# One copied score of every second phase is exponentiated on GpSimd, and the scores of a phase are dealt out anew

## The chip, the cores and the metric

The kernel runs on one core of a Trainium2 chip. The metric is the device time of one execution in microseconds (us); before the change it is 1262.92 us, the median of three runs (1262.78 to 1262.97).

## What is computed

A gate mixes two branches that read the same x (2048 tokens of 512 channels, float32):

```python
qkv = (x @ wqkv).reshape(B, S, 3, H, Dh)       # H = 32 heads, Dh = 16
p = softmax(einsum("bhqd,bhkd->bhqk", q, k) * Dh**-0.5)
a = einsum("bhqk,bhkd->bhqd", p, v).transpose(...).reshape(B, S, D) @ wo
u = gelu(einsum("bsd,sf->bdf", layernorm(x), w1) + b1)      # F = 1792
b = (einsum("bdf,fs->bds", u, w2) + b2).transpose(...)
out = g * a + (1 - g) * b                       # g = sigmoid((x * gate_w).sum(-1))
```

The attention needs 32 x 2048 x 2048 exponentials, and they are most of what follows.

## The kernel before, in words

**Ahead of the attention** come the projections, the layer norm and the first layer of the mixer branch. The change does not touch them.

**The attention** is a loop of 128 phases, p = 0 to 127, written out in the order in which each engine runs its work; no scheduler moves anything there. Four phases make a group: two heads against one half (1024) of the queries. The place of a phase in its group is called 0, 1, 2 or 3 here (`ph` in the code); places 1 and 3 are the `second` phases. A phase forms sixteen scores, each of 128 keys by 512 queries, numbered n = 0 to 15, and it has three stretches of TensorE work:

- sixteen score matmuls (L1067). Beside the first 14 (or 12) runs, on the other 64 rows of the array, half of a *dense* matmul (L1076) of other work: the second mixer layer, the queries of the second half (`late_query`), the output projection. Even phases do one half of these matmuls, odd phases the other, into one bank `dn`. A one-element GpSimd memset `token` (L1080), called the fence, stands between two phases: it waits for a phase's last dense matmul, and the next phase's first dense matmul waits for it.
- the last two scores, which run side by side without dense work.
- the matmuls with V (L963), which add all sixteen exponentiated scores into one PSUM bank `av`. VectorE then adds that bank to the running sum `ot` in SBUF (L985).

**Who takes a score out of PSUM.** Before the change, ScalarE exponentiates six scores one by one straight out of PSUM (`SINGLE`, n = 0, 2, 4, 6, 7, 9; L1093) and four in two pairs of 1024 columns (`TWO`; L1031). VectorE copies six (`EVAC`, n = 1, 3, 5, 8, 14, 15; L1089) into one SBUF tile `pe` of 3072 columns, and ScalarE exponentiates these in one instruction (L1102). The copied scores are used one phase later (`held`), the others in their own phase.

**Banks.** Seven PSUM banks go round for scores and `av`; the eighth is `dn`. A score matmul waits until the bank that it gets has been read. Worked through by hand, the rule `shares` gives this in all 128 phases: score 14 takes the bank of the fifth single (n = 7), score 15 that of the fourth copy (n = 8), and `av` that of the sixth single (n = 9).

**Sums at a group's edge.** In place 0, the held scores of the old group close its sum, and then the new group's first scores go to a second bank. VectorE adds the closing bank while the second is being filled; the second bank's addition stands at the head of the next phase, ahead of its copies.

**Around it on VectorE.** After its copies, an odd phase also empties a finished `dn` (L542, L816, or the five steps of `late_query`, L616 to L630), splits the next block of `w2` into a high part (`w_hi`, L67) and hands the low part to GpSimd (`w_lo`, L68, a subtraction of two SBUF tiles). Now and then come the reciprocals of the row sums (`inv`, L755 and L756) and the scaling and splitting of finished heads (`fetch`, `load_wo`, L1119 and L67/L68), most of them in the last sixteen phases.

The four lines that take scores out:

```python
nc.vector.tensor_copy(pt, s)                                              # L1089, EVAC
one = nc.scalar.activation(pt, s, AF.Exp, scale=SCALE)                    # L1093, SINGLE
pairs_done.append(nc.scalar.activation(pt, twos[low, low + 1], AF.Exp, scale=SCALE))   # L1031, TWO
done = nc.scalar.activation(x, x, AF.Exp, scale=SCALE)                    # L1102, the copied ones
```

Of the kernel before, what the change touches and what calls it, by code (L numbers as in the profile page):

```python
# [23 lines left out]
P = 128  # L24
# [33 lines left out]


@with_exitstack  # L60
def gated_mix(ctx: ExitStack, tc: tile.TileContext, a_x, a_wqkv, a_wo, b_w1, b_b1, b_w2, b_b2, gate_w, out):
# [38 lines left out]
    const.tile([P, 16], F32, name="pad")  # L100
# [501 lines left out]
    wq, between = [], {}  # L602

    def late_query(b, n):
# [9 lines left out]
        def begin():  # L614
            box.append(out_pool.tile([P, D], F32, name="row", bufs=3))
            nc.vector.tensor_copy(box[-1].bitcast(F32R), box[2])  # L616

        def out():
            ps, hi, cols = box[2], box[-1], slice((n - 2) * NB, (n - 1) * NB)
            lo, most_k = (out_pool.tile([P, D], F32, name="row", bufs=3) for _ in range(2))  # L620
            nc.vector.tensor_tensor(lo.bitcast(F32R), ps, hi, ALU.subtract)
            nc.vector.tensor_scalar(most_k, ps, most[:, b : b + 1], None, ALU.mult)
            nc.vector.tensor_reduce(qmax[:, b, n : n + 1], ps, axis=AX.X, op=ALU.max, apply_absolute_value=True)
            for i, t in enumerate((hi, lo)):
                nc.sync.dma_start(qp_d[1][b][i, :, cols], t)
            box.extend((most_k, qp_d[1][b][2, :, cols]))

        def finish():
            most_k, dst = box[-2:]
            nc.vector.scalar_tensor_tensor(most_k.bitcast(F32R), most_k, -1.0, most_k, ALU.mult, ALU.max)  # L630
            nc.sync.dma_start(dst, most_k)

        between[out] = begin
# [8 lines left out]
        return [(step, k, j) for k in range(ND) for j in range(3)], load, finish  # L642

    def second_layer(t):
# [3 lines left out]
        def step(fc, k):  # L648
            if fc == 0 and k == 0:
                box.append(ps_dn.tile([P, D], F32, name="dn"))  # L650
            if fc % 4 == 0 and k == 0:
                load_weight()
                box.append(ready.pop(0))
# [92 lines left out]
    def invert(half, k, pairs, at):  # L746
# [4 lines left out]
        t = out_pool.tile([P, w], F32, name="inv")[: n * DH]  # L751
# [97 lines left out]
    def put_whole(what, at):  # L849
        steps, load, *finish = what  # L850
        call(2 * at - 2, load)
        if finish:
            on_dve(2 * at + 2, *finish)
# [23 lines left out]
    for t in range(NS):  # L877
        at = put(second_layer(t), at, [14] * 3)
        if queries:
# [4 lines left out]
            if (b, n) == (ND - 1, 3):  # L884
                call(2 * at, open_wo)
                on_dve(2 * at + 1, greatest_of_all)
                call(2 * at + 2, bring_most)
                on_dve(2 * at + 4, least_shifts)
# [27 lines left out]
    token, mark = (out_pool.tile([1, 1], F32, name=name, bufs=1) for name in ("token", "mark"))  # L916

    EVAC = 1, 3, 5, 8, 14, 15
    SINGLE = 0, 2, 4, 6, 7, 9
    TWO = (10, 11), (12, 13)  # L920
    TURNS = [(0, 2), (4, 6), (7, 9), *TWO]
    HELD = [(1, 3), (5, 8), (14, 15)]

    def shares(n):

        for one in range(0, BANKS, 2):
            lows = [k for k in range(one)][::2] + [k for k in range(one + 1, BANKS)][::2]
            for third in lows:
                if n in (third, third + 1):
                    first, second = (low for low in lows if low != third)  # L930
                    return [first, first + 1, one, second, second + 1, 2 * third + 1 - n, n]


    def regions():
        return tc.tile_pool(name="ps_s", bufs=1, space=PSUM, reuse_waits="tile")
# [54 lines left out]
    with tc.manual_schedule(engines=engines):  # L990
        held, fence, turn, spare = [], None, 0, 0
        landed.clear()

        for p in range(LAST + 1):
# [17 lines left out]
            head = [second if n < n_b else (second + NSC - 1 - n) % 2 for n in range(NSC)]  # L1012
            if n_b == NSC - 2:
                head[-2:] = second, 1 - second
            else:
                head[-4:] = second, 1 - second, 1 - second, second
            in_turn = list(range(n_b)) + ([14, 15] if n_b == NSC - 2 else [12, 13, 15, 14])
# [9 lines left out]
            def exps(n):  # L1027
# [283 lines left out]
```

## Time and profile before

| what | value |
|---|---|
| median of three runs | 1262.92 us |
| the profiled execution's own time | 1262.86 us |
| its span in the profile | 1261.1 us |
| TensorE, busy share of the span | 99% |
| ScalarE, busy share | 85% |
| VectorE, busy share | 67% |
| GpSimd, busy share | 16% |
| granted TensorE clock | 1.0 |

The attention loop starts at 275.5 us of the span and its last score is formed at 1222 us, so it is three quarters of the time. In the stretch from 300 to 1100 us both TensorE and ScalarE are shown busy all the time. The ends of matmuls are modelled, and instructions of ScalarE overlap in the profile (the next is shown to start while the one before is still in the pipeline), so a share of 100% says only that an engine never stood empty; what it can do at most is read from the distance between the starts of its instructions.

### The profile page before, as it was taken

To read this page: it belongs to the slowest core of one execution; us is meant where nothing else is said; L and a number is where in the kernel's file an instruction comes from. 1 tells how busy PE (TensorE), PEld (TensorE's weight loads), DVE (VectorE), ACT (ScalarE), POOL (GpSimd) and SP (SyncE) were. 2 spreads that over 40 slices of the span, in tenths; PEclk is the share of its full clock that TensorE was granted. 3 is DMA by queue.
4 is the path that set the end of the run, shared out by engine and by line. 5 is a ranking of instruction groups with operands and counts; after the bars stand their busy time and mean duration, and the time that the engine had idled before them with its cause. 6 is when DMAs were issued, how large, how long until landed. Compare 5 with 4: busy or idle time off the path is not lost.

```text
span 1261.1 us, 32707 instructions
## 1 busy us (share of the span) xinstructions
PE 1253.0 (99%) x13342; PEld 827.9 (66%) x13342; DVE 850.8 (67%) x1562; ACT 1068.7 (85%) x1405; POOL 199.2 (16%) x316
## 2 busy tenths in 40 slices
PE   9999999999999999999999999999999999999998
PEld 7888888875666666666666666666666666666656
DVE  5675453178767676667667677776777677678883
ACT  4453343269999999999999999999999999999990
POOL 0220444561011101010110101111111111000000
PEclk9999999999999999999999999999999999999999
DMA  4799443253754443534344433444543443367621
GB/s 130 249 341 330 146 124 108 80 139 109 207 126 102 88 100 83 160 84 97 85 100 94 105 87 79 93 86 81 116 99 77 86 100 60 56 165 174 152 61 70
DMA packets 100555, 152.31 MB, mean 121 GB/s; under 512 B 17109, under 2 KB 56171, under 8 KB 96300
## 3 DMA queue, kind: packets, MB, share of 16 engines
q1 hardware_dynamic: 99820, 149.08, 46.6%
q8 instruction: 107, 1.75, 0.6%
q10 hardware_dynamic: 576, 1.05, 0.2%
q14 instruction: 52, 0.43, 0.1%
HBM read 105.39 MB, written 44.68 MB: 119 GB/s over the span
## 4 chain that ended last, share of the span: by engine, by line
PE 99%; ACT 1%; DVE 0%; issue 0%
PE av L963 32%; PE s L1067 23%; PE acc L424 12%; PE t L1067 9%; PE acc L75 8%; PE t L963 5%; PE u L1067 3%; PE dn L1076 3%; PE pa L1162 2%; PE acc L199 1%; PE acc L268 1%; PE acc L245 0%; ACT p L1093 0%; ACT pe L1102 0%; PE dn L1162 0%; PE pa L1192 0%
## 5 line engine op out<-in xcount | busy, mean ns | idle before, releaser
L1093 ACT ACTIVATE p<-s 128x512 f32<-128x512 f32 x768 | 412.3, 790 | 0.1
L1102 ACT ACTIVATE pe<-pe 128x3072 f32<-128x3072 f32 x129 | 381.8, 2962 | 0.0
L1067 PE MATMUL s<-qs,ks 64*128 64x512 f32 x1280 | 330.0, 400 | 0.6 <-ACT p L1093 0.6
L1089 DVE COPY pe<-s 128x512 f32<-128x512 f32 x512 | 318.1, 683 | 4.8 <-PE s L1067 0.8
L1067 PEld LDWEIGHTS s<-qs,ks 64*128 64x128 f32 x1280 | 225.6, 184 | 95.4 <-issue 45.3
L1031 ACT ACTIVATE p<-t 128x1024 f32<-128x1024 f32 x256 | 278.4, 1265 | 0.0
L963 PE MATMUL av<-p,v 128*32 128x256 f32 x3880 | 227.2, 379 | 0.0
L1089 DVE COPY pe<-u 128x512 f32<-128x512 f32 x256 | 164.8, 686 | 72.1 <-PE u L1067 72.1
L963 PE MATMUL av<-pe,v 128*32 128x256 f32 x3072 | 192.5, 383 | 0.0
L985 DVE TENSOR_TENSOR ot<-av,ot 128x512 f32<-128x512 f32 (+2 forms) x160 | 93.1, 582 | 141.5 <-PE av L963 140.2
L68 POOL TENSOR_TENSOR w_lo<-w_raw,w_hi 128x512 fp32r<-128x512 f32 (+1 forms) x128 | 153.5, 1206 | 194.5 <-ACT w_hi L67 101.8
L1076 PE MATMUL dn<-u_lo,w_hi 64*128 64x512 f32 x448 | 180.8, 404 | 0.0
L1076 PE MATMUL dn<-u_hi,w_hi 64*128 64x512 f32 x448 | 180.7, 403 | 0.0
L963 PEld LDWEIGHTS av<-p,v 128*32 128x32 f32 x3880 | 126.1, 110 | 83.2 <-ACT p L1093 0.2
L1076 PE MATMUL dn<-u_hi,w_lo 64*128 64x512 f32 x448 | 180.7, 403 | 0.0
L1067 PE MATMUL t<-qs,ks 64*128 64x512 f32 x512 | 142.5, 413 | 0.0
L963 PEld LDWEIGHTS av<-pe,v 128*32 128x32 f32 x3072 | 86.8, 109 | 82.1 <-ACT p L1093 37.8
L1080 POOL MEMSET token<- 1x1 f32 x128 | 11.3, 88 | 742.4 <-PE dn L1076 720.5
L67 ACT CAST w_hi<-w_raw 128x512 fp32r<-128x512 f32 (+1 forms) x67 | 38.0, 570 | 80.9 <-PE acc L424 59.4
L1067 PEld LDWEIGHTS t<-qs,ks 64*128 64x128 f32 x512 | 72.9, 184 | 51.2 <-ACT p L1093 49.9
L424 PE MATMUL acc<-h_hi,w_hi 128*128 128x512 f32 x224 | 87.1, 389 | 0.0
L424 PE MATMUL acc<-h_lo,w_hi 128*128 128x512 f32 x224 | 87.1, 389 | 0.0
(171 smaller groups left out, 1615.0 us busy)
## 6 DMA issues: line engine op xcount, KB each, us to landing
w_raw<-in_B_w_dram SPq DMA_DIRECT2D x96, 256.0 KB
ks<-kp SPq DMA_DIRECT2D x192, 128.0 KB
qs<-qp SPq DMA_DIRECT2D x256, 64.0 KB
kp<-pc SPq DMA_DIRECT2D x16, 512.0 KB
qp<-pc SPq DMA_DIRECT2D x8, 768.0 KB
qp<-row SPq DMA_DIRECT2D x24, 256.0 KB
v<-v SPq DMA_DIRECT2D x4, 1088.0 KB
x<-in_A_x_dram SPq DMA_DIRECT2D x16, 256.0 KB
```

The source lines that it names most:

```text
L67: copy(hi, src)
L68: return sub(lo, src, hi.bitcast(F32), ALU.subtract)
L75: nc.tensor.matmul(ps, a, b, start=start and n == 0, stop=stop and n == last)
L424: nc.tensor.matmul(p, a, b, start=first and k == 0, stop=last and k == 2)
L963: mm = nc.tensor.matmul(av[32 * j : 32 * (j + 1), i * QC : (i + 1) * QC], vb[b][:, v_at : v_at + 32], pt[:, h * QC : (h + 1) * QC], start= ...
L985: latest["add"] = nc.vector.tensor_tensor(x, y, x, ALU.add)
L1031: pairs_done.append(nc.scalar.activation(pt, twos[low, low + 1], AF.Exp, scale=SCALE))
L1067: nc.tensor.matmul(s, kt[grp][rows_i, c * P : (c + 1) * P], qt[grp][rows_i, qb * NB : (qb + 1) * NB], start=True, stop=True,)
L1076: mm = nc.tensor.matmul(ps, a[half], b[half], start=begin and not second, stop=last and bool(second))
L1089: nc.vector.tensor_copy(pt, s)
L1093: one = nc.scalar.activation(pt, s, AF.Exp, scale=SCALE)
L1102: done = nc.scalar.activation(x, x, AF.Exp, scale=SCALE)
```

## The change

It does five things.

1. **Shares.** `KINDS` deals the sixteen scores out as "sesesesseesessaa": ScalarE takes eight singles (n = 0, 2, 4, 6, 7, 10, 12, 13) and one pair (14, 15), VectorE six copies (n = 1, 3, 5, 8, 9, 11).
2. **GpSimd.** In even phases (`on_pool`), score 1 is not copied into `pe`. VectorE takes it out of PSUM scaled by log2(e)/4 into the tile `by` (L1159 of the changed kernel). GpSimd splits it into a whole and a broken part and builds 2 to the whole part from exponent bits (`powers`, four instructions), and after the fence begins a polynomial of the broken part (`polynomial`, six instructions). In the next, odd phase VectorE finishes it with two instructions that read two SBUF tiles each (`product`), after its copies, and the result goes to the V matmuls of that phase, in the last pair. ScalarE's instruction on the copied scores has 2560 columns in even phases and 3072 in odd ones.
3. **Banks** come from a table, `GIVEN`, one row a phase: the banks of the sixteen scores, then of `av`. Worked through by hand, all 128 rows give the following: the pair (14, 15) takes the banks of the fifth single (n = 7) and the fourth copy (n = 8), and `av` that of the sixth single (n = 10).
4. **Late queries.** VectorE copies the finished `dn` to SBUF at once, and the four other steps read that SBUF copy, spread over the next three phases.
5. **Small things.** `w_raw` has three buffers instead of four; three instructions around the bound of the scores are two phases later; `token` and `mark` lie elsewhere.

The diff, cut to its core:

```diff
-            raw = wk.tile([P, NB], F32, name="w_raw", bufs=4)
+            raw = wk.tile([P, NB], F32, name="w_raw", bufs=3)
...
         def out():
-            ps, hi, cols = box[2], box[-1], slice((n - 2) * NB, (n - 1) * NB)
-            lo, most_k = (out_pool.tile([P, D], F32, name="row", bufs=3) for _ in range(2))
-            nc.vector.tensor_tensor(lo.bitcast(F32R), ps, hi, ALU.subtract)
-            nc.vector.tensor_scalar(most_k, ps, most[:, b : b + 1], None, ALU.mult)
-            nc.vector.tensor_reduce(qmax[:, b, n : n + 1], ps, axis=AX.X, op=ALU.max, apply_absolute_value=True)
...
+            raw = out_pool.tile([P, D], F32, name="row", bufs=3)
+            nc.vector.tensor_copy(raw, box[2])
+            box.append(raw)
+
+        def high():
+            hi, most_k = (out_pool.tile([P, D], F32, name="row", bufs=3) for _ in range(2))
+            nc.vector.tensor_copy(hi.bitcast(F32R), box[3])
+            nc.vector.tensor_scalar(most_k, box[3], most[:, b : b + 1], None, ALU.mult)
+            box.extend((hi, most_k))
+
+        def greatest_query():
+            nc.vector.tensor_reduce(qmax[:, b, n : n + 1], box[3], axis=AX.X, op=ALU.max, apply_absolute_value=True)
+
+        def low():
+            raw, hi = box[3:5]
+            nc.vector.tensor_tensor(raw.bitcast(F32R), raw, hi, ALU.subtract)
...
-    EVAC = 1, 3, 5, 8, 14, 15
-    SINGLE = 0, 2, 4, 6, 7, 9
-    TWO = (10, 11), (12, 13)
...
+    KINDS = "sesesesseesessaa"
...
+    GIVEN = """
+    01234560123465013 64250163420561340 24165032145630125 43620153462015342
...
+        def powers():
+            nc.gpsimd.tensor_scalar(bt, by, 1.0, MAGIC + BIAS, ALU.mult, ALU.add)
+            nc.gpsimd.tensor_scalar(bg, bt, 1.0, MAGIC + BIAS, ALU.mult, ALU.subtract)
+            nc.gpsimd.tensor_tensor(bg, bg, by, ALU.subtract)
+            nc.gpsimd.tensor_scalar(bt.bitcast(I32), bt, 2.0**23, MAGIC * 2.0**23, ALU.mult, ALU.subtract)
+
+        def polynomial():
+            nc.gpsimd.tensor_scalar(by, bg, POWER2[5], POWER2[4], ALU.mult, ALU.add)
+            nc.gpsimd.tensor_tensor(by, by, bg, ALU.mult)
+            for k in (3, 2):
+                nc.gpsimd.tensor_scalar(by, by, 1.0, POWER2[k], ALU.mult, ALU.add)
+                nc.gpsimd.tensor_tensor(by, by, bg, ALU.mult)
+
+        def product():
+            nc.vector.scalar_tensor_tensor(by, by, POWER2[1], bg, ALU.add, ALU.mult)
+            return nc.vector.scalar_tensor_tensor(by, by, POWER2[0], bt, ALU.add, ALU.mult)
...
                     if n == n_b - 1:
                         fence = nc.gpsimd.memset(token, 0.0)
                         tc.add_manual_dep(fence.ins, mm.ins.name, SYNC, reason=REASON)
+                        if on_pool:
+                            polynomial()
...
+                if on_pool and n == EVAC[0]:
+                    nc.vector.tensor_scalar(by, s, SCALE * LOG2E, None, ALU.mult)
+                    powers()
+                    units[n] = i, c, qb, by
...
+            if second:
+                product()
             if n_b and second and beside[-1][-1]:
                 beside[-1][-1]()
...
-                apply_v(av, grp, held + turns, await_loads=ph == PHASES - 1)
+                if second:
+                    held, powered = held[1:], held[:1]
+                    apply_v(av, grp, held + turns + powered, await_loads=ph == PHASES - 1)
+                else:
+                    apply_v(av, grp, held + turns)
```

What it does to the order of instructions, at three places.

**GpSimd over two phases.** Before, GpSimd has two fences (`token`) and the low part of a weight block or two in each pair of phases:

```order
L1080 MEMSET token 1x1 x2
L68 TENSOR_TENSOR w_lo<-w_raw,w_hi 128x512
L68 TENSOR_TENSOR w_lo<-w_raw,w_hi 128x256
L1080 MEMSET token 1x1 x2
L68 TENSOR_TENSOR w_lo<-w_raw,w_hi 128x512
```

In the changed kernel (here phases 8 and 9), the tiles `bt`, `bg` and `by` hold the whole part, the broken part and the score, then the polynomial:

```order
L1063 TENSOR_SCALAR bt<-by 128x512
L1064 TENSOR_SCALAR bg<-bt 128x512
L1065 TENSOR_TENSOR bg<-bg,by 128x512
L1066 TENSOR_SCALAR bt<-bt 128x512
L1151 MEMSET token 1x1
L1069 TENSOR_SCALAR by<-bg 128x512
L1070 TENSOR_TENSOR by<-by,bg 128x512
L1072 TENSOR_SCALAR by<-by 128x512
L1073 TENSOR_TENSOR by<-by,bg 128x512
L1072 TENSOR_SCALAR by<-by 128x512
L1073 TENSOR_TENSOR by<-by,bg 128x512
L1151 MEMSET token 1x1
```

The first fence of the pair has four new instructions ahead of it in the queue, and the second fence has the whole polynomial ahead of it.

**VectorE from the end of a place 0 to the copies of the place 1 behind it.** Before (the end of phase 8 and the first copy of phase 9), the closing bank `av` takes two additions and the second bank, here named `t`, takes one:

```order
L1111 MEMSET mark 1x1
L630 SCALAR_TENSOR_TENSOR row<-row 128x512
L985 TENSOR_TENSOR ot<-av,ot 128x256
L985 TENSOR_TENSOR ot<-av,ot 64x256
L985 TENSOR_TENSOR ot<-t_3676,ot 128x256
L1089 COPY pe<-s_3755 128x512
```

In the changed kernel the closing bank takes one addition, and the second bank (`s_3778`) takes two:

```order
L1189 MEMSET mark 1x1
L629 CAST row<-row 128x512
L630 TENSOR_SCALAR row<-row,most 128x512
L1027 TENSOR_TENSOR ot<-s_3779,ot 128x256
L1027 TENSOR_TENSOR ot<-s_3778,ot 128x256
L1027 TENSOR_TENSOR ot<-s_3778,ot 64x256
L1164 COPY pe_3841<-s_3780 128x512
```

The second bank is full only at the end of the phase, so one more addition stands between that point and the next phase's first copy. This is so in 27 of the 32 groups; at the last four group edges the kernel before has two additions of the second bank as well, and the changed kernel has a single one of 128x512.

**VectorE from the last copy of phase 9 to its addition.** Before:

```order
L1089 COPY pe<-u_3804 128x512
L1089 COPY pe<-u_3805 128x512
L1111 MEMSET mark 1x1
L67 CAST w_hi<-w_raw 128x512
L67 CAST w_hi<-w_raw 128x256
L985 TENSOR_TENSOR ot<-av,ot 128x512
```

In the changed kernel, in one of the eight phases that also carry two steps of a late query (`row`):

```order
L1164 COPY pe_3841<-s_3893 128x512
L1076 SCALAR_TENSOR_TENSOR by<-by,bg 128x512
L1077 SCALAR_TENSOR_TENSOR by<-by,bt 128x512
L1189 MEMSET mark 1x1
L73 CAST w_hi<-w_raw 128x512
L73 CAST w_hi<-w_raw 128x256
L634 TENSOR_REDUCE z<-row 128x1
L638 TENSOR_TENSOR row<-row 128x512
L1027 TENSOR_TENSOR ot<-s_3917,ot 128x512
```

The two instructions of `product` stand ahead of the splitting of the weights, and the late query's subtraction of two SBUF tiles stands behind it, ahead of the addition that closes the phase.

More of the change, by code (lines that the diff above doesn't have):

```diff
@@ L98, in gated_mix @@
     rs = const.tile([P, NS], F32, name="rs")
-    const.tile([P, 16], F32, name="pad")
+    token, mark = (const.tile([1, 1], F32, name=name) for name in ("token", "mark"))
     upper = ctx.enter_context(tc.tile_pool(name="upper", bufs=1, side="right"))
@@ L600, in open_wo @@
         wo.extend(o_pool.tile([P, ND, D], F32R, name=f"big{i}") for i in range(2))
[L602 removed]
+    wq = []
     def late_query(b, n):
@@ L934, in regions @@
-    def regions():
-        return tc.tile_pool(name="ps_s", bufs=1, space=PSUM, reuse_waits="tile")
+    KINDS = "sesesesseesessaa"
+    SINGLES = 8
+    EVAC = [n for n, kind in enumerate(KINDS) if kind == "e"]
+    SINGLE = [n for n, kind in enumerate(KINDS) if kind == "s"]
+    TWO = [tuple(n for n, kind in enumerate(KINDS) if kind == two) for two in sorted(set(KINDS) - {"e", "s"})]
+    assert all(len(two) == 2 for two in TWO) and len(KINDS) == NSC
+    own = sorted([(n, n) for n in SINGLE] + [(two[1], n) for two in TWO for n in two])
@@ L1010, in gated_mix @@
             half = slice(0, HALF) if second else slice(HALF, P)
[L1012 to L1017, printed above, removed]
+            head = [second if n < n_b else (second + n - n_b) % 2 for n in range(NSC)]
             qbs = {}
```

188 lines of the change are left out of this document (114 added, 74 removed).

## The prediction

> **What bounds the kernel now.** I read the page first. Its shares leave two candidates for the bound, so I then laid the starts of ScalarE's instructions beside those of TensorE's, phase by phase.
>
> ```profile
> PE 1253.0 (99%) x13342; PEld 827.9 (66%) x13342; DVE 850.8 (67%) x1562; ACT 1068.7 (85%) x1405; POOL 199.2 (16%) x316
> ```
>
> The timeline of ScalarE in mid-loop (start, length, instruction, count):
>
> ```profile
> 603.42 3.24 ACT L1093 ACTIVATE p<-s 128x512 f32<-128x512 f32 x6
> 606.30 2.19 ACT L1031 ACTIVATE p<-t 128x1024 f32<-128x1024 f32 x2
> 608.14 3.00 ACT L1102 ACTIVATE pe<-pe 128x3072 f32<-128x3072 f32 x1
> 610.84 3.24 ACT L1093 ACTIVATE p<-s 128x512 f32<-128x512 f32 x6
> ```
>
> From one first single to the next are 610.84 - 603.42 = 7.42 us: that is a phase. By the distances of starts a single costs 2.88/6 = 0.48, a pair 1.84/2 = 0.92, the copied scores 2.70; together 7.42, no gap. Near the end of the loop the same engine reads differently:
>
> ```profile
> 1122.96 3.02 ACT L1093 ACTIVATE p<-s 128x512 f32<-128x512 f32 x6
> 1127.63 2.84 ACT L1102 ACTIVATE pe<-pe 128x3072 f32<-128x3072 f32 x1
> 1130.29 3.10 ACT L1093 ACTIVATE p<-s 128x512 f32<-128x512 f32 x6
> 1134.96 2.93 ACT L1102 ACTIVATE pe<-pe 128x3072 f32<-128x3072 f32 x1
> ```
>
> Here a phase lasts 1130.29 - 1122.96 = 7.33, but the instructions grow 0.08 to 0.09 longer from one phase to the next: a backlog builds up inside ScalarE. Its work in a phase is therefore 7.33 + 0.09 = 7.42, and ScalarE is what bounds the loop. The others can go at 7.33. What holds them there? First, the first score of five phases (112 to 116) on TensorE:
>
> ```profile
> 1107.33 0.50 PE L1067 MATMUL s<-qs,ks 64*128 64x512 f32 x1
> 1114.74 0.50 PE L1067 MATMUL s<-qs,ks 64*128 64x512 f32 x1
> 1122.39 0.50 PE L1067 MATMUL s<-qs,ks 64*128 64x512 f32 x1
> 1129.71 0.49 PE L1067 MATMUL s<-qs,ks 64*128 64x512 f32 x1
> 1137.04 0.49 PE L1067 MATMUL s<-qs,ks 64*128 64x512 f32 x1
> ```
>
> The periods are 7.41, 7.65, 7.32, 7.33. Then the weight loads of the last two scores (`u`) and of the V matmuls, in a phase of 7.42 and in one of 7.32 (in brackets: idle time, and who ended it):
>
> ```profile
> 613.63 0.19 PEld L1067 LDWEIGHTS u<-qs,ks 64*128 64x128 f32 x2 [0.19 <-ACT p L1093]
> 614.12 0.16 PEld L963 LDWEIGHTS av<-pe,v 128*32 128x32 f32 x8 [0.30 <-ACT p L1093]
> 1125.69 0.19 PEld L1067 LDWEIGHTS u<-qs,ks 64*128 64x128 f32 x2 [0.32 <-DVE pe L1089]
> 1126.12 0.16 PEld L963 LDWEIGHTS av<-pe,v 128*32 128x32 f32 x8 [0.24 <-ACT p L1093]
> ```
>
> Once ScalarE is not behind, VectorE's fourth copy holds the last two scores. And VectorE's additions and copies in the phases of 7.65 and of 7.32:
>
> ```profile
> 1114.94 0.86 DVE L985 TENSOR_TENSOR ot<-t,ot 128x256 f32<-128x256 f32 x2 [1.33 <-issue]
> 1115.83 2.48 DVE L1089 COPY pe<-s 128x512 f32<-128x512 f32 x4
> 1122.53 0.69 DVE L985 TENSOR_TENSOR ot<-av,ot 128x512 f32<-128x512 f32 x1 [1.55 <-PE av L963]
> 1123.16 2.48 DVE L1089 COPY pe<-s 128x512 f32<-128x512 f32 x4
> ```
>
> The first copy starts 1123.16 - 1122.39 = 0.77 after the phase's start, or, behind two additions of the second bank, 1115.83 - 1114.74 = 1.09 after it. These 0.32 are what the phase is longer: 7.65 against 7.32. So when ScalarE keeps up, the chain is first copy, fourth copy, last two scores, V matmuls, and VectorE's lateness goes one to one into the phase.
>
> **ScalarE's part of the change.** Eight singles and one pair cost 8 x 0.48 + 0.92 = 4.76. The copied scores cost 2.70 in an odd phase, 7.46 together. From 512 to 1024 columns an instruction grows by 0.44, so 2560 columns cost 2.26, an even phase 7.02. The mean is 7.24 where it was 7.42. Alone that would be 0.18 x 124 phases = 22 us.
>
> **What is late next.** By the table the last two scores still wait for the fifth single and the fourth copy, so a phase stays at 7.32 at least. The even phase's first copy is now a scaling. The rows of both kinds (behind the bar: busy us, mean ns of one, idle us before them), with a third that is used further down:
>
> ```profile
> L622 DVE TENSOR_SCALAR row<-dn,most 128x512 f32<-128x512 f32 x8 | 5.9, 742 | 0.0
> L542 DVE TENSOR_SCALAR row<-dn,b2x,omg 128x512 f32<-128x512 f32 x16 | 12.8, 802 | 0.0
> L1089 DVE COPY pe<-s 128x512 f32<-128x512 f32 x512 | 318.1, 683 | 4.8 <-PE s L1067 0.8 <-PE dn L1076 0.6
> ```
>
> A scaling out of PSUM is up to 0.06 longer than a copy: 0 to 0.06 in two phases of a group. After a place 3 ScalarE is 7.46 - 7.32 = 0.14 behind, worth 0 to 0.06 in place 0. And place 1 now begins with two additions of the second bank: 7.65. A group: 7.65 + 3 x 7.32 = 29.61, plus 0 to 0.18, against 4 x 7.42 = 29.68. I take 29.69, no change: 0 over 27 groups, within -2 and +3 us. At the last four edges the two additions go. Four phases there last 1137.04 - 1107.33 = 29.71 and become 4 x 7.32 + 0.1 = 29.4: -0.3 x 4 = -1.2 us. The first phases I leave at 0, within 1.
>
> **GpSimd's chain.** Undisturbed instructions on it, and two that differ only in reading an input (128x128):
>
> ```profile
> 601.06 1.29 POOL L68 TENSOR_TENSOR w_lo<-w_raw,w_hi 128x512 fp32r<-128x512 f32 x1 [1.78 <-DVE w_hi L67]
> 602.29 0.53 POOL L999 MEMSET ot<- 128x512 f32 x1
> masks.py:197 POOL MEMSET ident<- 128x128 f32 x1 | 0.2, 204 | 0.3 <-POOLq L1299 0.3
> masks.py:199 POOL TENSOR_SCALAR_AFFINE_SELECT ident<-ident 128x128 f32<-128x128 f32 x1 | 0.3, 292 | 0.0
> ```
>
> A two-input instruction is 1.3. No row shows the new one-input one: it lies between 0.53 and 1.3. By the nearest pair it is 0.292/0.204 x 0.53 = 0.76; I take 0.75. From the even phase's start, `by` is ready at 0.77 + 0.69 + 0.05 = 1.5, `powers` ends at 1.5 + 3 x 0.75 + 1.3 = 5.05, the fence follows, `polynomial` ends at 5.15 + 3 x 2.05 = 11.3, which is 4.0 into the odd phase. Both fences are done before the dense matmul that needs them (7.33). `product` has its place behind the sixth copy, at 0.77 + 6 x 0.6 = 4.4, and ends at 5.8. The V matmuls last 1129.71 - 1126.12 = 3.59, in sixteen steps of 0.22, and `by` is the last step but one: its result is due 0.55 before the phase's end, at 6.75. Nothing waits, with 0.95 to spare. `product` delays the emptying of `dn` (0.80 by L542) to 6.6, still ahead of 7.32; without that cover the next dense matmul would wait.
>
> **The crowded phases.** VectorE and GpSimd lock each other out:
>
> ```profile
> 942.34 1.80 DVE L1119 TENSOR_TENSOR row<-v,row 128x512 f32<-128x512 f32 x1
> 944.27 0.69 DVE L985 TENSOR_TENSOR ot<-av,ot 128x512 f32<-128x512 f32 x1
> 942.30 2.43 POOL L68 TENSOR_TENSOR w_lo<-w_raw,w_hi 128x512 fp32r<-128x512 f32 x2 [1.77 <-DVE w_hi L67]
> 1128.63 0.69 DVE L1119 TENSOR_TENSOR e<-o_sum,e 128x512 fp32r<-128x512 f32 x1
> 897.83 1.31 DVE L755 TENSOR_SCALAR inv<-inv 128x64 f32<-128x64 f32 x1
> 1129.24 0.19 DVE L755 TENSOR_SCALAR inv<-inv 128x64 f32<-128x64 f32 x1
> ```
>
> A subtraction or product of two SBUF tiles takes 0.69 alone and 1.80 beside GpSimd; a small scaling within SBUF 0.19 or 1.31. The addition of a PSUM bank (944.27) is not touched. Before, these steps came early enough to end ahead of the phase. Now `product` (1.4) stands ahead of them in odd phases, and GpSimd is at its polynomial in even ones. Other rows used:
>
> ```profile
> 941.80 0.42 DVE L67 CAST w_hi<-w_raw 128x512 fp32r<-128x512 f32 x1
> 1129.46 0.55 DVE L756 RECIPROCAL inv<-inv 128x64 f32<-128x64 f32 x1
> L67 DVE CAST w_hi<-w_raw 128x512 fp32r<-128x512 f32 x45 | 19.0, 422 | 0.0
> ```
>
> - Late queries, eight phases in place 1. Copies end at 1.09 + 3.6 = 4.7, `product` at 6.1, GpSimd's `w_lo` begins 0.5 after the cast (942.30 - 941.80) and ends at 6.6 + 1.3 = 7.9. The late query's subtraction waits for that and leaves at 8.45. The phase's addition, due at 7.65 + 0.14, is 0.66 late, the next first copy about 0.6: 4.8 us.
> - Reciprocals in six phases of place 3 (19, 35, 51, 67, 83, 99): `product` to 5.8, GpSimd 6.3 to 7.6, then 0.1 and 0.55 lead to 8.2 where 7.46 is due: 0.75, once over 1.3 (phase 99 empties `dn` too); 0.8 x 6 = 4.8.
> - Products of `fetch` in phases 85, 89, 101, 105: as the first kind, once 1.3: 0.8 x 4 = 3.2.
> - Even phases 70, 114, 118, 122, 126, three or four such steps each, 1.7 to 3.1 long, from 4.4 on. Each may wait for one instruction of the polynomial (mean of 0.75 and 1.3: 1.0): with 3.0 of room, 1.0 to 2.7 over; I take 1.7 x 5 = 8.5.
>
> Together 21.3. The last term is the least certain: the rows show the lock against GpSimd's two-input instruction only. If one-input ones do not lock, it is half, and the sum 4 us less; I take the full one, since the row at hand is nearer to a lock than to none. The Trainium skill ("SBUF — State Buffer", Who interferes with whom) names any GpSimd instruction that reads SBUF, so by that rule the full price stands; the rows at 942 and 897 agree as far as they go. One buffer of `w_raw` less costs nothing as long as loads run a block ahead of the casts (0.0 idle before L67); without that cover, a cast is late in some odd phases. Where `token` and `mark` lie, and the three steps that come two phases later, are on no chain: 0.
>
> **Sum.** 0 - 1.2 + 21.3 = +20.1 on the profiled execution's 1262.86 (span 1261.1; the median of the runs is 1262.92): **1283.0 us**. With the crowded phases at half or at one and a half, 1270 to 1296.
>
> **Rivals.**
> - *GpSimd becomes the bound* (slower still). `polynomial` must end 12.7 after the even phase's start, so that `product` can end by 6.75; this leaves 11.1 for ten instructions, 5.9 for six one-input ones: 0.98 each decides. At 1.15 the pair of phases lasts 1.5 + 0.1 + 5.2 + 6.9 + 1.4 + 0.55 = 15.65, 1.0 too long, x 63: about 1346; just over the limit 1300. For it: nothing shows the instruction. Against: 0.76. Chance 0.13. The Trainium skill ("GPSIMD Engine Reference", Elementwise — side-by-side cycle accounting) gives 769 ns for 512 elements in a tight loop, so by an estimate from it the limit holds; no run here shows it yet.
> - *VectorE's room swallows the crowded phases*: it is busy 67%. Then only -1.2 is left, 1261.7, within 0.2% of 1262.9, which is about what a measurement of this kernel can tell from no change. Against it: in exactly those phases the room is used up. 0.13.
> - *Faster*: ScalarE's relief arrives after all, because score 15 gets its bank earlier behind the two additions than the phase of 7.65 shows. Place 1 at 7.32 makes a group 29.3, -0.37 x 27 = -10, with the crowded phases swallowed 1251.6; it decides where place 1 stays under 7.4. Against it: 7.65 is measured with the same two additions. 0.12.
>
> **Numbers.** My forecast 0.62, GpSimd as the bound 0.13, no change 0.13, faster 0.12. So slower by over 0.2%: 0.75; within 0.2%: 0.13; faster by over 0.2%: 0.12. The range from 1259 to 1305 takes in the forecast's own range, the flat case and the near edges of the two others; what lies outside is most of the faster case and the slower part of GpSimd's, together about 0.2.
>
> **What would show it.** ScalarE's singles short (2.9 to 3.1 for six) with idle time at the start of phases; the periods 7.35, 7.65, 7.35, 7.32 in quiet groups; the last two scores released by VectorE; `product` without a wait; periods over 8 behind the phases named. Wrong if quiet groups last under 29.4 or over 30, if `product` waits for GpSimd, or if no period behind a crowded phase is over 7.8.

## The result and the profile after

| | median of the runs, us | range | ratio to the kernel before (95%) |
|---|---|---|---|
| before, same session | 1262.85 | 1262.78 to 1262.97 (4) | 1 |
| changed | 1372.3 | 1371.87 to 1372.9 (4) | 1.0867 (1.0848 to 1.0886) |

The forecast was 1283.0, its range 1259 to 1305: the sign is right, the size is not. The profiled execution of the changed kernel took 1371.87 us, its span is 1370.0, 108.9 more than before. Of these, 105.5 lie in the attention loop from its first score to the first score of the last phase (1048.9 for 943.4), 1.7 ahead of it and 1.6 behind it.

The shares of the whole span, from the page:

```profile
PE 1294.0 (94%) x13342; PEld 876.5 (64%) x13342; DVE 968.8 (71%) x1691; ACT 1072.4 (78%) x1533; POOL 939.1 (69%) x956
```

No engine is full any more. GpSimd grew from 199 to 939 us, and its 69% would not make it a suspect. The chain of work that ended last says more:

```profile
POOL 47%; PE 29%; DVE 11%; issue 7%; DMA 3%; SPq 2%; ACT 1%; POOLq 0%; DVEq 0%; ACTq 0%
```

ScalarE's singles of the phases 38 to 41 (in brackets: idle time ahead, and what ended it):

```profile
591.93 4.03 ACT L1168 ACTIVATE p<-s 128x512 f32<-128x512 f32 x8 [0.78 <-PE s L1138]
599.54 4.03 ACT L1168 ACTIVATE p<-s 128x512 f32<-128x512 f32 x8 [0.45 <-PE s L1138]
607.96 4.03 ACT L1168 ACTIVATE p<-s 128x512 f32<-128x512 f32 x8 [0.84 <-PE s L1138]
615.37 4.19 ACT L1168 ACTIVATE p<-s 128x512 f32<-128x512 f32 x8 [0.24 <-PE s L1138]
```

ScalarE now stands idle at each phase's head, and phases last 7.61, 8.42 and 7.41, where all were 7.42. The groups of GpSimd's instructions in the loop (behind the bar: busy us, mean ns of one, idle us before them):

```profile
L1073 POOL TENSOR_TENSOR by<-by,bg 128x512 f32<-128x512 f32 x126 | 162.6, 1291 | 10.5
L1066 POOL TENSOR_SCALAR bt<-bt 128x512 int32<-128x512 f32 x63 | 131.9, 2094 | 0.0
L1064 POOL TENSOR_SCALAR bg<-bt 128x512 f32<-128x512 f32 x63 | 121.3, 1925 | 5.2
...
L1072 POOL TENSOR_SCALAR by<-by 128x512 f32<-128x512 f32 x125 | 77.5, 620 | 10.9
...
L1069 POOL TENSOR_SCALAR by<-bg 128x512 f32<-128x512 f32 x63 | 39.4, 626 | 5.1
L1063 POOL TENSOR_SCALAR bt<-by 128x512 f32<-128x512 f32 x63 | 39.2, 622 | 73.9 <-DVE by L1159 73.3
```

Two kinds of one-input instructions stand there. Four of the six take 0.62, below the 0.75 of the forecast. The other two, L1064 and L1066, take 1.93 and 2.09 in the mean; they are the two that multiply and *subtract*. The six come to 6.5 us, 1.09 each, where the forecast had put the limit at 0.98. One pair of phases in time:

```profile
605.38 0.69 DVE L1076 SCALAR_TENSOR_TENSOR by<-by,bg 128x512 f32<-128x512 f32 x1 [1.93 <-POOL token L1151]
606.11 0.69 DVE L1077 SCALAR_TENSOR_TENSOR by<-by,bt 128x512 f32<-128x512 f32 x1
...
606.85 0.11 PEld L1005 LDWEIGHTS s<-by,v 128*32 128x32 f32 x2 [1.27 <-DVE by L1077]
...
608.19 0.69 DVE L1159 TENSOR_SCALAR by<-s 128x512 f32<-128x512 f32 x1
...
608.97 0.62 POOL L1063 TENSOR_SCALAR bt<-by 128x512 f32<-128x512 f32 x1 [3.11 <-DVE by L1159]
609.67 1.92 POOL L1064 TENSOR_SCALAR bg<-bt 128x512 f32<-128x512 f32 x1
...
620.02 1.29 POOL L1073 TENSOR_TENSOR by<-by,bg 128x512 f32<-128x512 f32 x1
...
621.25 0.09 POOL L1151 MEMSET token<- 1x1 f32 x1
621.34 0.69 DVE L1076 SCALAR_TENSOR_TENSOR by<-by,bg 128x512 f32<-128x512 f32 x1 [1.78 <-POOL token L1151]
```

It is a ring. The scaled score (608.19) lets GpSimd begin; ten instructions and the fence last from 608.97 to 621.34, 12.37 us; VectorE's product has waited 1.78 for them; behind it TensorE's weight load of `by` has waited too (606.85, 1.27); and the end of that phase lets the next scaled score begin. The product is named as waiting for `token`, since the fence is what GpSimd ran last; what it needs is the polynomial in front of it. From product to product are 621.34 - 605.38 = 15.96 us, for two phases that were 14.83. The waits over the loop (us in total, times, longest):

```profile
DVE by L1076 <- POOL token L1151: 111.1, 60, 2.0
...
POOL bt L1063 <- DVE by L1159: 73.3, 33, 4.7
PEld s L1005 <- DVE by L1077: 45.7, 40, 1.3
```

The 33 times at the second row are worth a look: GpSimd still stands idle for up to 4.7 us in half of its pairs of phases, and yet it sets the pace. In the eight pairs with a late query, 17.6 us long, the next scaled score comes late behind the delayed product and the late query's steps on VectorE.

The 1.7 us ahead of the loop have a cause of their own. The chain at that place (start, length, what):

```profile
268.92 1.24 POOL w_lo L74
...
270.18 2.79 DMA w_raw<-in_B_w_dram
...
273.07 0.62 ACT w_hi L73
273.69 0.53 ACT u_hi L450
...
274.24 1.38 DVE u_lo L452
...
275.72 1.42 DVE row L555 x2
...
277.19 0.49 PE s L1138
```

With three buffers of `w_raw`, a load can start only when GpSimd has finished with the block three before (270.16), and its 2.79 us then stand open ahead of ScalarE's casts and all that follows, up to the loop's first score at 277.19. Before, with four buffers, that score started at 275.47 and the chain there is TensorE alone.

### The profile page after: what moved, and what is told of

Read it like the earlier page. It is cut to its first block, busy times and chain, and to the rows that moved or that the text cites. A ratio compares the mean times of both kernels' runs of the same rounds, so it can differ in the third digit from the quotient of the medians.

```text
span 1370.0 us, 33370 instructions
## 1 busy us (share of the span) xinstructions
PE 1294.0 (94%) x13342; PEld 876.5 (64%) x13342; DVE 968.8 (71%) x1691; ACT 1072.4 (78%) x1533; POOL 939.1 (69%) x956
## 4 chain that ended last, share of the span: by engine, by line
POOL 47%; PE 29%; DVE 11%; issue 7%; DMA 3%; SPq 2%; ACT 1%; POOLq 0%; DVEq 0%; ACTq 0%
PE acc L430 11%; POOL by L1073 9%; POOL bt L1066 8%; POOL bg L1064 8%; PE acc L81 8%; POOL bg L1065 5%; POOL by L1070 5%; POOL by L1072 5%; PE dn L1147 3%; POOL bt L1063 3%; PE s L1005 3%; DVE by L1076 2%; POOL by L1069 2%; DMA qs<-qp 2%; PE s L1138 2%
## 5 line engine op out<-in xcount | busy, mean ns | idle before, releaser
L1138 PE MATMUL s<-qs,ks 64*128 64x512 f32 x1792 | 469.2, 406 | 14.3 <-DVE ot L1027 10.6
L1164 DVE COPY pe<-s 128x512 f32<-128x512 f32 x704 | 432.3, 682 | 8.0 <-PE s L1138 7.2
L1178 ACT ACTIVATE pe<-pe 128x2560 f32<-128x2560 f32 (+1 forms) x129 | 334.4, 2593 | 0.0
L1005 PE MATMUL s<-p,v 128*32 128x256 f32 x5120 | 299.7, 379 | 0.0
L1005 PEld LDWEIGHTS s<-p,v 128*32 128x32 f32 x5120 | 166.4, 110 | 109.8 <-issue 0.2
L1005 PE MATMUL s<-pe,v 128*32 128x256 f32 x2816 | 204.7, 384 | 0.0
L1073 POOL TENSOR_TENSOR by<-by,bg 128x512 f32<-128x512 f32 x128 | 165.2, 1291 | 10.7
L1116 ACT ACTIVATE p<-t 128x1024 f32<-128x1024 f32 x128 | 138.6, 1083 | 0.0
L1066 POOL TENSOR_SCALAR bt<-bt 128x512 int32<-128x512 f32 x64 | 134.3, 2098 | 0.0
L1064 POOL TENSOR_SCALAR bg<-bt 128x512 f32<-128x512 f32 x64 | 123.2, 1925 | 5.3
```

The source lines that it names most:

```text
L1005: mm = nc.tensor.matmul(av[32 * j : 32 * (j + 1), i * QC : (i + 1) * QC], vb[b][:, v_at : v_at + 32], pt[:, h * QC : (h + 1) * QC], start= ...
L1064: nc.gpsimd.tensor_scalar(bg, bt, 1.0, MAGIC + BIAS, ALU.mult, ALU.subtract)
L1066: nc.gpsimd.tensor_scalar(bt.bitcast(I32), bt, 2.0**23, MAGIC * 2.0**23, ALU.mult, ALU.subtract)
L1073: nc.gpsimd.tensor_tensor(by, by, bg, ALU.mult)
L1116: pairs_done.append(nc.scalar.activation(pt, open_two, AF.Exp, scale=SCALE))
L1138: nc.tensor.matmul(s, kt[grp][rows_i, c * P : (c + 1) * P], qt[grp][rows_i, qb * NB : (qb + 1) * NB], start=True, stop=True,)
```

## The experiments

My theory after the result: two of GpSimd's one-input instructions are slow because of *subtract* as the second operation; this alone makes GpSimd the bound, as the first rival describes it. What else could make them slow is the integer output of the second one, or VectorE locking GpSimd out. Each ratio below is to the kernel before, run on the same chip beside it (1262.9 to 1263.1 us). The length of a phase is the distance from its first score to the next phase's first score, read from the trace.

**Add a negative constant.** x - c is written as x + (-c) in both lines:

```diff
-            nc.gpsimd.tensor_scalar(bg, bt, 1.0, MAGIC + BIAS, ALU.mult, ALU.subtract)
+            nc.gpsimd.tensor_scalar(bg, bt, 1.0, -(MAGIC + BIAS), ALU.mult, ALU.add)
...
-            nc.gpsimd.tensor_scalar(bt.bitcast(I32), bt, 2.0**23, MAGIC * 2.0**23, ALU.mult, ALU.subtract)
+            nc.gpsimd.tensor_scalar(bt.bitcast(I32), bt, 2.0**23, -MAGIC * 2.0**23, ALU.mult, ALU.add)
```

> Edit: the two GpSimd instructions that multiply and then subtract a constant (L1064 and L1066) multiply and add the negative constant instead; the same numbers come out. In the changed kernel the four one-input instructions that multiply and add take 0.62 us each, these two 1.92 and 2.10, and product waits 1.85 us for GpSimd in each pair of phases. Theory A (the pair of operations multiply-subtract is slow on GpSimd): both fall to 0.6 to 0.7, the ten instructions go from 12.3 to 9.7 us, product waits no more, and the time falls to what was forecast with a chain that fits: 1272 to 1295. Rival B (the numbers, beyond 2**23, or the integer output make them slow): both stay at 1.9 and 2.1, 1372 stays. Rival C (the lock between VectorE and GpSimd in the crowded phases made most of the loss): the two get short, but the time stays over 1320.

Measured: 1285.83 us (1285.22 to 1288.41), ratio 1.0187 (1.0170 to 1.0204). The two groups, and GpSimd's own wait:

```profile
L1064 POOL TENSOR_SCALAR bg<-bt 128x512 f32<-128x512 f32 x64 | 39.7, 620 | 5.3
L1066 POOL TENSOR_SCALAR bt<-bt 128x512 int32<-128x512 f32 x64 | 39.7, 620 | 0.0
```

```profile
POOL bt L1063 <- DVE by L1159: 116.5, 64, 5.8
```

Both take 0.62 now, with the integer output too, so neither that output nor a lock was the price. No wait of the product for GpSimd is left among the large ones, and GpSimd waits for VectorE in all 64 pairs: it is off the path. That is 86.5 us of the 109.5; the other 23 are the subject of all further runs.

**Only the first of the two lines.**

```diff
-            nc.gpsimd.tensor_scalar(bg, bt, 1.0, MAGIC + BIAS, ALU.mult, ALU.subtract)
+            nc.gpsimd.tensor_scalar(bg, bt, 1.0, -(MAGIC + BIAS), ALU.mult, ALU.add)
```

> Edit: as e1_add_negative, in L1064 alone (float32 in and out); L1066 (integer output) keeps multiply-subtract. Theory A: L1064 0.62, L1066 stays at 2.10; the ten instructions take 11.0, at the limit of 11.1 that was worked out, so most of the wait is gone: 1280 to 1310. Rival B by the integer output alone: the same picture for L1064, but then L1066 stays at 2.1 in e1_add_negative too. Rival B by the large numbers: L1064 stays at 1.92 and the time at 1372.

Measured: 1293.35 (1293.14 to 1294.17), ratio 1.0241 (1.0224 to 1.0258). The line that was left, and the product's wait:

```profile
L1066 POOL TENSOR_SCALAR bt<-bt 128x512 int32<-128x512 f32 x64 | 123.9, 1936 | 0.0
```

```profile
DVE by L1076 <- POOL token L1151: 29.7, 60, 1.5
```

One slow instruction, 1.3 us longer, costs 7.5 us in all; the second costs 79. That is a limit being crossed and not a sum: with one of them the chain just about fits into two phases.

**Without GpSimd's exponential.** Shares, banks and late queries stay as changed; ScalarE exponentiates the copied score 1 with the others, and there is no product.

```diff
-            on_pool = not second
+            on_pool = False
...
-            if second:
-                product()
```

> Edit: the new shares, banks and late queries alone; score 1 is copied in even phases too, GpSimd forms no exponential and VectorE no product, ScalarE's copied scores have 3072 columns in every phase. ScalarE's work is 7.46 a phase against 7.42 before: + 0.04 x 124 = 5 us, and behind the two additions at a group's edge up to 0.2 more in 27 groups. Theory A (all of the loss beyond this is GpSimd's chain and product): 1266 to 1274. Rival (the new bank table or the spread late queries cost by themselves): over 1280.

Measured: 1273.8 (1272.63 to 1274.23), ratio 1.0084 (1.0067 to 1.0101). So the new shares, banks and late queries together cost 10.7 us, and GpSimd's exponential, once it fits, 12.0 more. ScalarE's singles of the phases 45 to 47:

```profile
615.11 4.21 ACT L1167 ACTIVATE p<-s 128x512 f32<-128x512 f32 x8
...
622.79 4.03 ACT L1167 ACTIVATE p<-s 128x512 f32<-128x512 f32 x8
...
630.21 4.09 ACT L1167 ACTIVATE p<-s 128x512 f32<-128x512 f32 x8
```

Phase 45, in place 1, lasts 622.79 - 615.11 = 7.68, and the one behind it 630.21 - 622.79 = 7.42. In all the quiet groups place 1 lasts 7.69 in the mean and the others 7.42: 27 x 0.27 = 7.3 of the 10.7 are there.

**One addition at the edge.** The kernel of the first experiment, without the second bank's addition of 64x256, so that a part of the running sums `ot` is left out:

```diff
+        if not final and len(parts) == 2:
+            parts = parts[:1]
```

> Edit: as e1_add_negative, and the second addition of the second bank at each group's edge (64 rows by 256 columns) is left out, so part of each sum lacks the first phase's share. If, with GpSimd out of the way, the fourth copy sets the phase, place 1 loses its 0.32: about 28 x 0.32 = 9 us less than e1_add_negative. If ScalarE or GpSimd sets it, the two are within 2 us of each other.

Measured: 1277.89 (1277.04 to 1280.59), ratio 1.0124 (1.0107 to 1.0141), 7.9 less than with it; place 1 lasts 7.42 like the rest. The longer place 1 is that addition ahead of the first copy.

**The pair two scores earlier.** The kernel of the first experiment with another deal of the scores. The table of banks is new too, and ScalarE's instruction on the copied scores now depends on the pair, where it depended on the last single:

```diff
-    KINDS = "sesesesseesessaa"
+    KINDS = "sesesesseeseaass"
```

> Edit: e1_add_negative with the pair at scores 12 and 13 and singles at 14 and 15, and a bank table written anew by the same rule (score 14 still takes the fifth single's bank, 15 the fourth copy's, the pair those of the third copy and the fourth single). In e1_add_negative the fourth copy ends 3.25 us after a phase's start, but the weights of the last two scores load at 3.37 to 3.40, and quiet phases last 7.42 instead of the forecast 7.32. Theory D: the pair is one tile, its first matmul waits for two engines, and the second wait costs 0.1. Then scores 14 and 15, each with one wait, load at about 3.30, quiet phases last 7.32, place 1 about 7.6, and the time falls by 8 to 13 us to 1273 to 1278. Rival E: ScalarE's fifth single, which the profile names, is really late; then score 14 still waits for it, 7.42 stays, and the time is within 3 us of e1_add_negative.

Measured: 1281.24 (1279.64 to 1281.89), ratio 1.0142 (1.0125 to 1.0159): 4.6 less, about half of what was expected. TensorE's weight loads at the end of phase 47 with the pair last, behind ScalarE's first single of that phase:

```profile
634.41 4.03 ACT L1168 ACTIVATE p<-s 128x512 f32<-128x512 f32 x8 [0.26 <-PE s L1138]
...
637.25 0.22 PEld L1138 LDWEIGHTS t<-qs,ks 64*128 64x128 f32 x2 [0.48 <-ACT p L1168]
637.72 0.16 PEld L1005 LDWEIGHTS s<-pe,v 128*32 128x32 f32 x8 [0.24 <-ACT p L1168]
```

The same phase with the pair earlier:

```profile
633.34 3.05 ACT L1168 ACTIVATE p<-s 128x512 f32<-128x512 f32 x6
...
635.95 0.34 PEld L1138 LDWEIGHTS s<-qs,ks 64*128 64x128 f32 x2 [0.16 <-ACT p L1168]
636.54 0.16 PEld L1005 LDWEIGHTS s<-pe,v 128*32 128x32 f32 x8 [0.25 <-ACT p L1168]
```

From the first single to the first V weights are 637.72 - 634.41 = 3.31 with the pair last and 636.54 - 633.34 = 3.20 with two singles last, and the phase goes from 7.43 to 7.33. My reading: a pair at the end must have both of its banks, of which one is read by ScalarE and one by VectorE, before either half can start, and two singles start each by itself. In even phases the gain is missing (7.44): there ScalarE, behind by its 3072 columns of the odd phase, begins late (its first single starts 0.74 behind the phase's first score there, 0.53 in odd phases).

**One addition, with all the sums.** Score 15 is copied, so that more of the sums are held and the second bank needs one addition, of 128x256, as before the change (the closing bank takes two); nothing is left out. The table of banks is new here as well:

```diff
-    KINDS = "sesesesseeseaass"
+    KINDS = "sesesesseessaase"
```

> Edit: as e5_pair_earlier, and the last copied score is 15 instead of 11 (singles at 10, 11 and 14), so that the second bank at a group's edge takes one addition and the closing bank two, as in the kernel before. Place 1 then starts its first copy at 0.77 instead of 1.04 and should last 7.32 instead of 7.6: 27 x 0.27 = 7 us less than e5_pair_earlier, 1266 to 1271. If the addition is not what makes place 1 long, the two are within 2 us of each other.

Measured: 1273.24 (1273.00 to 1274.09), ratio 1.0083 (1.0067 to 1.0100), 8.0 less. ScalarE's singles of the phases 44 to 48:

```profile
607.99 3.62 ACT L1168 ACTIVATE p<-s 128x512 f32<-128x512 f32 x7
...
615.29 3.54 ACT L1168 ACTIVATE p<-s 128x512 f32<-128x512 f32 x7
...
622.69 3.62 ACT L1168 ACTIVATE p<-s 128x512 f32<-128x512 f32 x7
...
629.99 3.54 ACT L1168 ACTIVATE p<-s 128x512 f32<-128x512 f32 x7
...
637.39 3.13 ACT L1168 ACTIVATE p<-s 128x512 f32<-128x512 f32 x6
```

Four phases last 637.39 - 607.99 = 29.40, where they were 29.67 before the change. This is the relief of ScalarE that the change is able to give: 0.27 a group, 7 us a kernel. The crowded phases and the first ones eat it.

**Crowded pairs without GpSimd.** In fourteen pairs of phases, named by their even phase in the diff, ScalarE exponentiates `by` by itself, and `powers`, `polynomial` and `product` are left out:

```diff
+    PLAIN = (0, 2, 66, 70, 82, 88, 100) + tuple(range(114, 128, 2))
...
+            if on_pool and p in PLAIN:
+                nc.scalar.activation(by, by, AF.Exp, scale=SCALE)
```

> Edit: as e6_one_edge_addition, but in the pairs of phases from 0, 2, 66, 70, 82, 88, 100 and from 114 on (crowded ones) ScalarE exponentiates score 1 in an instruction of its own and GpSimd and product are left out. The phases behind crowded ones that lasted 7.8 to 9.4 in e1_add_negative should come down to 7.4 to 7.6: 6 to 11 us less than e6_one_edge_addition, 1257 to 1263. If crowding on VectorE is not what made them long, no change or up to 5 us more for ScalarE's extra work.

Measured: 1264.01 (1263.33 to 1265.62), ratio 1.0008 (0.9999 to 1.0018): 9.2 less, and even with the kernel before. The phases 68, 71 and 115 go from 8.36, 9.30 and 8.62 to 7.40, 7.63 and 7.46. Not all of the gain is theirs: in the two profiles the loop is 7.8 shorter, and 1.4 of that lie in the phases 0 to 4.

**The late queries' pairs too.**

```diff
-    PLAIN = (0, 2, 66, 70, 82, 88, 100) + tuple(range(114, 128, 2))
+    PLAIN = (0, 2, 66, 70, 82, 88, 100) + tuple(range(114, 128, 2)) + tuple(range(8, 65, 8))
```

> Edit: as e7_plain_crowded, and the eight pairs with a late query (from phases 8, 16, ... 64) are plain too. They cost 0.49 each in e1_add_negative, 4 us; ScalarE's extra half microsecond takes up to 0.36 a pair back: 1 to 4 us less than e7_plain_crowded, or the same.

Measured: 1264.74 (1263.74 to 1265.82), ratio 1.0014 (1.0004 to 1.0023). No gain that the times show. A pair without GpSimd lasts 7.56 + 7.48 where it was 7.32 + 7.87, so 0.15 less, and 1.2 less in eight pairs. In the two profiles the loop is 0.9 shorter (943.0 for 944.0), but the work behind it is 1.2 longer (43.3 for 42.1), and no run shows why; the ranges of the two kernels overlap.

**The late query's subtraction one phase later.** In the rows of the first experiment, at the end of phase 41 (start, length), the late query's subtraction (L638) runs past the phase's end:

```profile
594.95 2.44 POOL L74 TENSOR_TENSOR w_lo<-w_raw,w_hi 128x512 fp32r<-128x512 f32 x2 [2.59 <-DVE w_hi L73]
...
595.70 1.09 DVE L638 TENSOR_TENSOR row<-row 128x512 fp32r<-128x512 f32 x1
...
596.04 0.49 PE L1138 MATMUL s<-qs,ks 64*128 64x512 f32 x1
...
596.71 0.68 DVE L1027 TENSOR_TENSOR ot<-s,ot 128x512 f32<-128x512 f32 x1
```

The new phase's first score starts at 596.04, and the old phase's addition, ahead of the new phase's first copy, only at 596.71. Against the seventh kernel:

```diff
-        return [(step, k, j) for k in range(ND) for j in range(3)], load, (high,), (greatest_query, low), (finish,)
+        return [(step, k, j) for k in range(ND) for j in range(3)], load, (high,), (greatest_query,), (low,), (finish,)
```

> The kernel of e7, with the late query's subtraction of two SBUF tiles (the low part, with its two DMAs) moved from the odd phase of place 1 into the even phase behind it; its last step is one phase later too. Theory: the 0.48 that the phase behind each of eight late queries is longer (7.86 for 7.38) comes from this subtraction, which stands behind the product and the weight splitting and waits for GpSimd's low weight part ahead of the addition that closes the phase. In the even phase there is no product, so it has room: 8 x 0.48 = 3.9 less, 1260.1 us, and the eight phases at 7.38. Rival: it locks against GpSimd's polynomial there, and the even phase's addition is late instead: 1264, with the phase after place 2 (7.32) at 7.6 to 8. A second rival: what is late in the odd phase is the greatest query's reduction, which stays; then the eight phases stay at 7.86 and the time at 1264.

Measured: 1266.1 (1264.8 to 1269.38), ratio 1.0027 (1.0017 to 1.0037). The eight phases came down from 7.86 to 7.38 as forecast, but the last step, moved along with it, now stood in the odd phases 19, 35 and 51 beside the reciprocals; the phases behind those rose from 7.38 to 8.28, 8.75 and 8.74, and phase 71 from 7.63 to 9.60. So the kernel is 2.1 us slower than the seventh, where 3.9 less had been expected.

**Subtraction and last step in the even phase.** Against the seventh kernel as well:

```diff
-        return [(step, k, j) for k in range(ND) for j in range(3)], load, (high,), (greatest_query, low), (finish,)
+        return [(step, k, j) for k in range(ND) for j in range(3)], load, (high,), (greatest_query,), (low, finish)
```

> The kernel of e9_low_one_phase_later, with the late query's last step back in the phase where e7 has it, so that it stands right behind the subtraction, both in the even phase. In e9 the eight phases behind late queries came down to 7.38 as forecast, but three phases (20, 36, 52) rose from 7.38 to 8.28, 8.75 and 8.74, and one (71) from 7.63 to 9.60. Theory: the first three rose because the last step then stood in the odd phase with the reciprocals, the fourth because the bound of the scores came later by one phase through the last step's transfer; all four go back, 0.9 + 1.4 + 1.4 + 2.0 = 5.6 less than e9's 1266.1: 1260.5 us, 0.2% under the kernel before. The late start (277.4 for 275.5) stays. Rival: subtraction and last step together are too much for the even phase beside the polynomial, and its closing addition is late: the phase behind it at 7.8 or more, the time at 1264.

Measured: 1260.25 (1259.16 to 1261.38), ratio 0.9979 (0.9970 to 0.9988). This is 2.6 us less than the kernel before the change, 0.2%, and no run of the one lies in the range of the other. The three phases are back at 7.38, phase 71 at 7.75, the eight stay at 7.38. The loop lasts 939.9 for 943.4; 1.7 of the 3.4 that it gains are lost ahead of it to the third buffer of `w_raw`. That loss is read off the chain, where the same load stands open for 2.69 in this kernel too (270.22, the first score at 277.13), and no run shows it by itself. The ninth kernel with four buffers, and with phase 0 back on GpSimd, was expected at 1257 to 1258, but it has no time: its tiles do not fit into SBUF (the pool `ot` needs 6.25 KB a partition, and 4.25 are left).

## Why the prediction was wrong

Point by point, with the first experiment (1283.5 us of span, 22.4 over the kernel before) for what lies beside the failed step. The period of each phase is the distance of its first score to the next phase's.

| step | forecast, us | measured, us |
|---|---|---|
| GpSimd's chain | 0 | +86.5 (changed kernel against the first experiment) |
| quiet groups, 27 edges | 0 | +7.2: place 1 7.68 for 7.42 |
| last four edges | -1.2 | -0.9, and +0.5 in the phases between |
| first phases (0 to 4) | 0 | +1.8 |
| `w_raw`'s third buffer | 0 | +1.6 |
| late queries | 4.8 | 3.9: eight phases 7.91 for 7.42 |
| reciprocals, six | 4.8 | 1.2: two phases, 68 and 84; four cost nothing |
| `fetch`, four | 3.2 | 1.0: two phases, 90 and 102; two cost nothing |
| even phases | 8.5 | 5.3: 71, 115, 119, 123 |
| not foreseen | | +0.5 in phase 116, +0.4 behind the loop |

1. **The step that failed** is the price of GpSimd's one-input instruction: "No row shows the new one-input one: it lies between 0.53 and 1.3. By the nearest pair it is 0.292/0.204 x 0.53 = 0.76; I take 0.75." Four of the six come out below that (0.62). I priced six instructions as one kind, though the diff shows two pairs of operations; multiply and subtract takes 1.93 and 2.09, outside the bounds, since the upper bound was the two-input row and nothing says that one input is cheaper whatever the operation. The pair that I scaled by was no better: a memset and an affine select differ in the operation too, and not only in reading an input. The sign that I had named for this came: `product` waits for GpSimd, 60 times in the loop.
2. **The rival was the right mechanism.** The limit was put as "5.9 for six one-input ones: 0.98 each decides"; the mean of 1.09 is over it, and the ring through polynomial, product and V matmuls sets the pace as described. Its price was too low: at 1.09 its own sum gives 1.5 + 0.1 + 5.2 + 6.5 + 1.4 + 0.55 = 15.25 for a pair of phases, and 15.96 were measured. GpSimd's ten instructions add up to 11.7, and last 12.37 with the fence: between two that depend on each other 0.08 are lost (609.67 - 608.97 - 0.62), which the sum left out.
3. **Quiet groups.** I let place 1 be 7.65 and the other three 7.32 to 7.38, and these cancelled against 7.42. Place 1 came (7.68); the other three stayed at 7.42, by my reading since the pair at the end waits for two engines. The fifth and sixth experiments take these two apart: 7.32 appears once the pair is earlier, and place 1 falls to 7.32 with one addition. That the wait for two engines itself is what takes the 0.1 is read from the rows and was not tried apart from the pair's place.
4. **Crowded phases** are real: the seventh experiment takes GpSimd out of those without a late query, and of the first phases, and gains 9.2. Their places were mostly those named, but they cost 11.4 us in all and not 21.3: I took every step within SBUF as caught by GpSimd for a full instruction, and in six of the ten phases with reciprocals or `fetch` nothing was late.
5. **The cover that I named was missing.** "One buffer of `w_raw` less costs nothing as long as loads run a block ahead of the casts": I had looked at the casts inside the loop, and the cost is at the loop's start, where no load runs ahead.

Without the failed step the sum would have been near (1283.0 against 1285.8), but by errors that cancel: quiet phases, edges, start and buffer some 12 too cheap, crowded phases 10 too dear.

## What to carry to other kernels

Price each new instruction by its operation and not only by its shape and engine: where no row has that operation, an upper bound from another kind of instruction is no bound. A chain across engines that returns once per period has a limit and not a price: below it a slow instruction costs nothing or little (7.5 us for one), above it every extra microsecond is paid every period (79 us for the second), so work out how far it is from the limit, with the gaps between dependent instructions. When an engine is relieved, look at which wait ends last next, and be wary of an instruction there that needs two engines' results (the rows of the fifth experiment point to it, and no run shows it by itself).

## What the runs showed of the hardware

- On GpSimd, a multiply and a subtraction with two constants on 128x512 took 1.93 us, and the same with an addition of the negative constant 0.62. With int32 output they took 2.09 and 0.62 in the mean. The 2.09 holds two kinds: 33 of the 64 took 1.91 to 1.93, and the other 31, 2.09 to 3.20, began while VectorE had a longer instruction on SBUF tiles under way. So the integer output cost nothing, and the two engines hold each other up. One of the undisturbed ones in the changed kernel:

```profile
646.52 1.92 POOL L1066 TENSOR_SCALAR bt<-bt 128x512 int32<-128x512 f32 x1
```

  Which part of the engine is slow there, no run shows. The Trainium skill ("GPSIMD Engine Reference", Elementwise — side-by-side cycle accounting) has 769 ns for 512 elements in a tight loop. The addition is below that here, and the subtraction takes 2.5 times as long; that section does not tell the two apart.
- GpSimd holds VectorE up with one-input instructions as well. The late query's cast within SBUF, eight of them, first in the eighth kernel (no GpSimd exponential in these phases), then in the first experiment and in the changed kernel:

```profile
L629 DVE CAST row<-row 128x512 fp32r<-128x512 f32 x8 | 3.4, 423 | 0.0
```

```profile
L629 DVE CAST row<-row 128x512 fp32r<-128x512 f32 x8 | 6.1, 756 | 0.0
```

```profile
L629 DVE CAST row<-row 128x512 fp32r<-128x512 f32 x8 | 11.7, 1457 | 0.0
```

  The means are 0.42 alone, 0.76 where the one-input L1066 was under way when the cast began, and 1.46 where it was the two-input L1065, each time in all eight. The open point of the forecast, whether one-input instructions lock, is thereby answered with yes. The Trainium skill ("SBUF — State Buffer", Who interferes with whom) names casts among the VectorE instructions that can contend with GpSimd, and these rows agree.
